# First MLP's low words partly by identity products, one spread for two, and new offsets in a fused attention and two-MLP kernel

## The chip, the cores and the metric

The kernel runs on one core of a Trainium2 chip. The metric is the device time of one execution in microseconds, as a median of several runs. The engines are PE (TensorE, matrix products; PEld is its loading of weights), DVE (VectorE), ACT (ScalarE), POOL (GpSimd) and SP (SyncE, which issues most DMAs).

## The reference

Three layers stand one behind another, for 4 batches of 768 tokens and 384 columns (8 heads of 48):

```python
# 1. delta-rule attention, token by token
k_n = k / (norm(k) + 1e-6)
for t in range(S):
    y[t] = q[t] @ state
    state += beta[t] * outer(k_n[t], v[t] - k_n[t] @ state)
# 2. first MLP: a low-rank mixing of the tokens, then 384 -> 1536 -> 384
u = x + (x.T @ U @ V).T
x = u + maximum(u @ w_ch1, 0) @ w_ch2
# 3. second MLP: real part of a 2-d Fourier transform, layer norm, the same MLP
u = x + real(fft(fft(x, axis=1), axis=2))
x = u + maximum(layernorm(u) @ w_ch1, 0) @ w_ch2
```

All is float32. The kernel keeps that accuracy with pairs of f16 words: a value is a high word and a low word, and a product is three products (high with high, high with low, low with high).

## The kernel before

The kernel has no schedule of its own in its source. Each part is a generator (a stream) that yields the cost and the engine of its next operation before it issues it, and a planner, `Weave`, picks at build time among all streams the one whose next operation can start first by its model, with an offset for each stream (`PR0`, `PR`, `P2`, `ME`, `MX`, `MB0`, `MB` and the like) and a price for each engine (`PRICE`, `PRICE2`). The order of issue on each engine is therefore fixed when the kernel is built, and each engine works through its own list in that order. The planner's clocks `free["v"]`, `free["a"]`, `free["p"]` say when DVE, ACT and PE would be done with what was issued so far. `SPW` is an addition to the time that a DMA issue waits for another engine's result.

There are two phases. In `attention` the sequence is cut into 24 chunks (4 batches of 6 chunks of 128 tokens). For a chunk, `s_front` and `row_scales` scale keys and queries (with `norm` for the reciprocal root), `s_turn` transposes them by DMA, `s_prep_a` makes the products of keys with keys and queries, `s_split` splits them into words, `s_prep_b` (two lanes) and `s_prep_c` invert a triangular matrix block by block, and `s_solve` carries the state from chunk to chunk. `s_solve` posts ("sol", u) when chunk u is done; its result, vt, is written at L1087.

Beside this the streams of the first MLP run whenever they fit: `s_mix` (the low-rank mixing and the split into words), `s_moe1` (the MLP) and `s_out1`. What is left of them goes on into the second phase, `second`, with the transform (`s_fft`), the second MLP's weights and the second MLP (`s_moe2`).

Both MLPs are `s_mlp` (`wi` is 0 for the first one and 1 for the second). A tile has 384 tokens; there are 8 tiles and 12 steps for each, so 96 steps in each MLP. In a step, nine products of 384 columns (L1135) fill a bank ps_h in PSUM; ACT writes the high word hh = Relu(ps_h) (L1141); DVE writes the low word hl = max(ps_h, 0) - hh (L1148); and nine products (L1165) take the words of the step before into three banks acc. In the first MLP ps_h has a single bank, so the next step's first product waits for hl.

`spread` (L827) multiplies a compact matrix, repeated along the columns, by a mask: the tiles t (T02 and T11, 512 columns each) in `s_prep_c`, bd and nf (1024 columns) elsewhere. In `s_prep_c` T02 is used in the products ps_l, and T11, after a block of it was replaced, in ps_x. `norm` has on DVE a line for s0 times a factor plus a summand (L657) between a product (L655) and the sum s1 (L660). `s_split` has, for the first 8 chunks, what the change brings to the MLP: the products with a negative identity, idm, onto the bank (L813) and a second ACT pass over it (L815), which leaves the low word.

Of the kernel before, what the change touches and what calls it, by code (L numbers as in the profile page):

```python
# [9 lines left out]
F32 = mybir.dt.float32  # L10
F32R = mybir.dt.float32r
F16 = mybir.dt.float16
BF16 = mybir.dt.bfloat16
U32 = mybir.dt.uint32
ALU = mybir.AluOpType
ACTF = mybir.ActivationFunctionType
# [3 lines left out]
B, H, S, D = 4, 8, 768, 48  # L20
DM = 384
DFF = 1536
NC = S // 128
# [17 lines left out]
NP = 27  # L41
UA = 8
SPARE = 150.0
SPW = 0.0
PR0 = (-272, -129.0, -103.0, 119.0, -13, -79, 889, 238.0)
PR = (-20.0, -145.0, -187.0, -178, 362, 14.0, 310, -190)
ME = -49
MX = -607
MB = -561
MB0 = -600.0  # L50
P2 = (-261, 79, -1288, -22, -199, -243, 152, -346)
MP = 29
WB1 = -697
WB = -409
PRICE0 = {'p': 1.0, 'v': 3.16, 'a': 0.82, 'g': 0.1}
PRICE = {'p': 1.0, 'v': 0.35, 'a': 0.57, 'g': 0.19}
PRICE2 = {'p': 1.0, 'v': 4.28, 'a': 0.53, 'g': 0.45}
SC = 16.0
CQ, CV, CW, CF = 6, 10, 9, 9
CU = 5  # L60
# [134 lines left out]
def _v(n, rate=1):  # L195
    return 67 + n / (0.96 * rate)


def _a(n, psum=False):
    return (51 if psum else 93) + n / 1.2  # L200
# [10 lines left out]
class Builder:  # L211
# [306 lines left out]
    def attn_pools(self, ctx):  # L518
        tc, nc = self.tc, self.nc
        self.psb = ctx.enter_context(tc.tile_pool(name="psb", bufs=1, space=PSUM))  # L520
        self.psr = ctx.enter_context(tc.tile_pool(name="psr", bufs=1, space=PSUM))
        self.pss = ctx.enter_context(tc.tile_pool(name="pss", bufs=1, space=PSUM))
        self.ap1 = ctx.enter_context(tc.tile_pool(name="ap1", bufs=1))
        self.ap2 = ctx.enter_context(tc.tile_pool(name="ap2", bufs=2))

        kq = self.kq0 = self.ap1.tile([128, 2, H, D], F32, tag="kq", name="kq", bufs=NQ)
        for i, src in enumerate((self.k, self.q)):
            nc.sync.dma_start(kq[:, i], src[0, :, 0:128, :].rearrange("h p d -> p h d"))
        self.mask2 = self.ap1.tile([128, 128], F32, name="mask2")
        nc.sync.dma_start(self.mask2, self.cmask)  # L530
        mm = self.ap1.tile([128, 640], F16, name="mmask")
        nc.gpsimd.dma_start(mm, self.cmerge)
        self.mpair, self.mcol, self.mdiag = mm[:, 0:32], mm[:, 32:64], mm[:, 64:96]
        self.mbd = mm[:, 96:224].rearrange("p (j c) -> p j c", j=4)
        self.mlev = [mm[:, x:x + 128].rearrange("p (j c) -> p j c", j=4) for x in (224, 352)]
        self.mt02, self.mt11 = (mm[:, x:x + 64].rearrange("p (j c) -> p j c", j=2) for x in (480, 544))
        self.betaT = self.ap1.tile([128, B * H * NC], F32, name="betaT")
        bv = self.beta.rearrange("b h (c p) -> (b h c) p", p=128)
        for i in range(2):
            bst = self.keep.tile([128, 128], F32, tag="xn", name="bst", bufs=TB // 128)  # L540
            nc.sync.dma_start(bst[0:96], bv[96 * i:96 * i + 96, :])
            pt = self.psm.tile([128, 512], F32, tag="psm", name="ps_b")
            nc.tensor.transpose(pt[:, 0:96], bst[0:96, :], self.id32[0:96, 0:96])
            nc.vector.tensor_copy(out=self.betaT[:, 96 * i:96 * i + 96], in_=pt[:, 0:96])

        def zeros(n, shape, nm):
            ts = [self.ap1.tile(shape, F16, name=f"{nm}{i}") for i in range(n)]
            for t in ts:
                (nc.vector if nm[0] == "k" else nc.gpsimd).memset(t, 0.0)
            return ts  # L550

        self.id16 = self.ap1.tile([128, 128], F16, name="id16")
        nc.vector.tensor_copy(out=self.id16, in_=self.id32)
        self.ids = self.ap1.tile([128, 128], F16, name="ids")
        nc.vector.tensor_scalar(out=self.ids, in0=self.id32, scalar1=SC, scalar2=None, op0=ALU.mult)
        self.idm = self.ap1.tile([128, 128], F16, name="idm")
        nc.vector.tensor_scalar(out=self.idm, in0=self.id32, scalar1=-1.0, scalar2=None, op0=ALU.mult)

        self.kq16 = zeros(NQ, [128, 2, H, 2, 64], "kq16")
        self.kb16r = zeros(NK, [128, H, 2, 64], "kb16")  # L560
        self.Nfr = [self.ap1.tile([128, H, 128], F16, name=f"nf{i}") for i in range(NR)]
        self.bd = [self.ap1.tile([128, H, 128], F16, name=f"bd{i}") for i in range(4)]
        self.T02, self.T11 = (self.ap1.tile([128, H, 64], F16, name=f"t1{i}") for i in range(2))
        self.lanes = self.psb.tile([128, 2, H, 32], F32, name="lanes")
        self.X128 = zeros(1, [128, H, 64], "t")[0]
        self.Xm = zeros(1, [128, H, 32], "xm")[0]
# [78 lines left out]
    def norm(self, pool, ss, n, eps, scale=1.0):  # L645

        nc = self.nc
        s0 = pool.tile([128, n], F32, tag="n_s0", name="n_s0", bufs=1)
        yield {"a": 190}
        nc.scalar.activation(out=s0, in_=ss, func=ACTF.Sqrt, bias=self.tiny)  # L650
        t = pool.tile([128, n], F32, tag="n_t", name="n_t", bufs=1)
        yield {"v": 76}
        nc.vector.reciprocal(out=t, in_=s0)
        yield {"v": 76}
        nc.vector.tensor_tensor(out=t, in0=ss, in1=t, op=ALU.mult)  # L655
        yield {"v": 76}
        nc.vector.tensor_scalar(out=s0, in0=s0, scalar1=0.5 / scale, scalar2=eps / scale, op0=ALU.mult, op1=ALU.add)  # L657
        s1 = pool.tile([128, n], F32, tag="n_s1", name="n_s1", bufs=NK + 2 if pool is self.ap2 else 2)
        yield {"v": 76}
        nc.vector.scalar_tensor_tensor(out=s1, in0=t, scalar=0.5 / scale, in1=s0, op0=ALU.mult, op1=ALU.add)  # L660
        r1 = pool.tile([128, n], F32, tag="n_r1", name="n_r1")
        yield {"v": 76}
        nc.vector.reciprocal(out=r1, in_=s1)
        return s1, r1
# [230 lines left out]

    def s_prep_c(self):
        nc = self.nc
        T02, T11, X128, Xm = self.T02, self.T11, self.X128, self.Xm
        Q = [slice(32 * i, 32 * i + 32) for i in range(4)]
        for u, _ in self.each():  # L900
            yield ("b", u)
# [2 lines left out]
            GPh = self.un[u]["GPh"]  # L904
            Tc, Nc = self.un[u].pop("TN")
            Nf = self.Nfr[u % NR]
            yield from self.spread(T02, Tc, self.mt02)
            t = yield from self.take()
            ps = self.psu.tile([128, H, 64], F32, tag="psu", name="ps_l")
            yield self.pe(H, 64)  # L910
# [7 lines left out]
            t = yield from self.take()  # L918
            pz = self.psu.tile([128, H, 32], F32, tag="psu", name="ps_z")
            yield self.pe(H, 32)  # L920
            for h in range(H):
                nc.tensor.matmul(pz[:, h, :], Nf[:, h, :], Xm[:, h, :], start=True, stop=True)
            yield from self.spread(T11, Tc, self.mt11)
            self.wv.post("ce", u)
            Zs = self.ap2.tile([128, H, 32], F16, tag="Zs", name="Zs", bufs=1)
            yield from self.cp(Zs, pz, 256, "chain", psum=True)
# [5 lines left out]
            t = yield from self.take()  # L932
            ps = self.psu.tile([128, H, 64], F32, tag="psu", name="ps_x")
# [177 lines left out]
    def s_mlp(self, wi, count, n_, np_, psm):  # L1111
# [5 lines left out]
        for s in range(count * steps + 1):  # L1117
            n, p = divmod(s, steps)
            if n < count:
                if p == 0:  # L1120
                    yield ("u", wi, n)
                    u = self.u[wi, n]
                pool, tag = psm[s % len(psm)]
                ps = pool.tile([128, np_, n_], F32, tag=tag, name="ps_h")
                for i in range(np_):
                    f = np_ * p + i
                    yield ("weights", wi, "w1", f // 3)
                    w1h, w1l = self.wt[wi, "w1h", f // 3], self.wt[wi, "w1l", f // 3]
                    fs = slice(128 * (f % 3), 128 * (f % 3) + 128)
                    m = 0  # L1130
                    for k in range(KD):
                        if k % MG == 0:
                            yield {"q": 3 * MG * (n_ / 2.4 + 2.5)}, "par"
                        for w, x in ((w1h, 0), (w1h, 1), (w1l, 0)):
                            nc.tensor.matmul(ps[:, i, :], w[:, k, fs], u[x][:, k, :], start=(m == 0), stop=(m == 3 * KD - 1))  # L1135
                            m += 1
                yield "join"
                hh = self.keep.tile([128, np_, n_], F16, tag="hh", name="hh", bufs=2)
                hl = self.keep.tile([128, np_, n_], F16, tag="hl", name="hl", bufs=2)
                yield {"a": _a(np_ * n_, True)}, "side"  # L1140
                nc.scalar.activation(out=hh, in_=ps, func=ACTF.Relu)  # L1141
            if pend and pend[0][1] == 0:
                ac = []
            for i in range(np_):
                for d in range(KD):
                    if n < count and i * KD + d == (np_ * KD // 3 if pend else 0):
                        yield {"v": _v(np_ * n_)}, "side"
                        nc.vector.scalar_tensor_tensor(out=hl, in0=ps, scalar=0.0, in1=hh, op0=ALU.max, op1=ALU.subtract)  # L1148
                    if not pend:
                        continue  # L1150
                    pn, f, xh, xl = pend[i]
# [526 lines left out]
```

## Time and profile before

| | us |
|---|---|
| median of 3 runs | 1105.74 (1100.96 to 1106.52) |
| profiled execution, its own time | 1102.48 |
| its span, first to last instruction | 1100.7 |
| PE busy | 945.0 (86%) |
| DVE busy | 747.5 (68%) |
| ACT busy | 555.1 (50%) |
| POOL busy | 330.0 (30%) |
| mean granted PE clock | 0.944 |

The shares are means over stages that differ, so they are read by stretch. Products on PE are pipelined: the duration of one in a table is longer than the distance to the next one. A granted clock of 1.00 is 2.4 GHz and one of 0.50 is 1.2 GHz; a mean between them is a share of time at either.

### The profile page before, as it was taken

Reading aid. Unit: us, or ns where it says so; the run is one execution under the profiler, and the core shown is the slowest. Engines: PE = TensorE matmul, PEld = TensorE weight load, DVE = VectorE, ACT = ScalarE, POOL = GpSimd, SP = SyncE. Lnnn points to the kernel's source line nnn. Section 1 sums busy time; section 2 is a strip of 40 time slices with the busy share of each in tenths; the row PEclk is TensorE's granted clock in tenths of the full one; section 3 lists DMA queues with packets and bytes.
Section 4 is the critical chain, followed back from the end, with each engine's and each line's share of the span. In section 5 each row is a group of like instructions: output and inputs, shape, how many; then the busy total and the mean of one; then the engine's idle time right before and its main releaser. Section 6 shows DMA issues by size and latency. Waiting matters only on the chain. (4 is left out here: it accounts for less than half of the span.)

```text
span 1100.7 us, 25252 instructions
## 1 busy us (share of the span) xinstructions
PE 945.0 (86%) x10127; PEld 633.1 (58%) x10127; DVE 747.5 (68%) x1735; ACT 555.1 (50%) x1372; POOL 330.0 (30%) x320
## 2 busy tenths in 40 slices
PE   0477776679999989998999889789999999999998
PEld 0255555446666656665666456455767575665665
DVE  7678689778989889897886377764425543544432
ACT  5589797766665655675553144356522221222221
POOL 4231323015343223543410450355353612102010
PEclk9998796579999999999999899899999999999999
DMA  9987976518555395476312455531102211212210
GB/s 229 221 172 151 203 159 139 122 41 150 115 102 110 86 181 118 86 147 121 71 38 66 131 154 142 150 94 29 56 11 67 78 29 37 65 29 58 58 37 22
DMA packets 226142, 112.18 MB, mean 102 GB/s; under 512 B 194396, under 2 KB 214184, under 8 KB 226024
## 3 DMA queue, kind: packets, MB, share of 16 engines
q1 hardware_dynamic: 223576, 103.32, 42.6%
q0 software_dynamic: 2448, 7.24, 2.2%
q8 instruction: 79, 1.29, 0.5%
q14 instruction: 39, 0.32, 0.1%
HBM read 55.63 MB, written 14.16 MB: 63 GB/s over the span
## 5 line engine op out<-in xcount | busy, mean ns | idle before, releaser
L1165 PE MATMUL acc<-w2s,hh 128*128 128x384 f16 x1152 | 288.2, 333 | 0.0
L1135 PEld LDWEIGHTS <-w1s 128*128 128x128 f16 x1728 | 164.5, 99 | 125.8 <-issue 24.7
L1148 DVE SCALAR_TENSOR_TENSOR hl<-ps_h,hh 128x384 f16<-128x384 f32 x192 | 106.1, 553 | 178.8 <-ACT hh L1141 176.7
L1141 ACT ACTIVATE hh<-ps_h 128x384 f16<-128x384 f32 x192 | 94.0, 489 | 241.7 <-PE ps_h L1135 238.7
L1165 PE MATMUL acc<-w2s,hl 128*128 128x384 f16 x576 | 190.9, 331 | 3.2 <-DVE hl L1148 3.2
L1135 PE MATMUL ps_h<-u,w1s 128*128 128x384 f16 x864 | 174.9, 336 | 21.3 <-DVE hl L1148 16.0
L1135 PE MATMUL ps_h<-uh,w1s 128*128 128x384 f16 x864 | 157.5, 326 | 0.0
L1165 PEld LDWEIGHTS <-hh 128*128 128x128 f16 x1152 | 108.7, 100 | 63.6 <-issue 4.6
L248 POOL TENSOR_TENSOR GPl<-g,GPh 128x512 f16<-128x512 f32 x63 | 79.6, 1264 | 172.2 <-ACT GPh L241 167.3
L847 PEld LDWEIGHTS <-bd 128*128 128x128 f16 x1728 | 71.9, 99 | 55.7 <-DVE bd L827 21.5
L1165 PEld LDWEIGHTS <-hl 128*128 128x128 f16 x576 | 57.2, 99 | 43.3 <-DVE hl L1148 4.0
L780 PE MATMUL ps_g<-K,BT 128*128 128x256 f16 x192 | 57.0, 316 | 17.1 <-DMA K<-KT 17.1
L779 PE MATMUL ps_g<-KT,BT 128*128 128x256 f16 x192 | 56.2, 309 | 14.0 <-ACT GPl L815 6.9
L248 POOL TENSOR_TENSOR pair<-x1f,pair 128x384 f16<-128x384 f32 x24 | 21.9, 915 | 132.1 <-ACT pair L1524 132.1
L786 DVE TENSOR_TENSOR g<-ps_g,mask 128x512 f32<-128x512 f32 x64 | 43.6, 682 | 11.1 <-PE ps_g L780 9.9
L248 POOL TENSOR_TENSOR pm<-xq 97x768 f32<-97x768 f32 (+1 forms) x16 | 28.8, 1816 | 65.2 <-DVE u L1296 45.9
L241 ACT ACTIVATE GPh<-g 128x512 f16<-128x512 f32 x61 | 38.0, 625 | 19.4 <-DVE g L786 19.1
L248 POOL TENSOR_TENSOR kb<-kq,rb 128x384 f32<-128x384 f32 x22 | 18.6, 846 | 91.6 <-ACT rh L1013 26.5
L780 PEld LDWEIGHTS <-BT 128*128 128x128 f16 x192 | 20.5, 107 | 36.8 <-DMA K<-KT 19.1
L827 DVE TENSOR_TENSOR bd<-Xc,mmask 128x1024 f16<-128x1024 f16 x48 | 36.8, 769 | 6.9 <-ACT Xc L881 6.5
L248 POOL TENSOR_TENSOR kq<-kq,kq 128x384 f16<-128x384 f32 x43 | 40.5, 962 | 3.3 <-ACT GPh L241 1.7
L847 PE MATMUL lanes<-R,bd 128*128 128x32 f16 x768 | 35.1, 180 | 5.5 <-ACT R L241 2.9
(261 smaller groups left out, 1927.1 us busy)
## 6 DMA issues: line engine op xcount, KB each, us to landing
wst<-in_moe_w_ch_dram SPq DMA_DIRECT2D x51, 384.0 KB
K<-KT SPq DMA_DIRECT2D x48, 256.0 KB
kq<-in_k_dram SPq DMA_DIRECT2D x24, 192.0 KB
kq<-in_q_dram SPq DMA_DIRECT2D x24, 192.0 KB
vt<-in_v_dram SPq DMA_DIRECT2D x24, 192.0 KB
xnd<-vt SPq DMA_DIRECT2D x24, 192.0 KB
xn<-xnd SPq DMA_DIRECT2D x24, 192.0 KB
x1d<-u SPq DMA_DIRECT2D x24, 192.0 KB
```

What stands on the lines that cost most here:

```text
L241: self.nc.scalar.activation(out=out, in_=in_, func=ACTF.Copy)
L248: (self.nc.vector if eng == "v" else self.nc.gpsimd).tensor_tensor(out=out, in0=in0, in1=in1, op=op)
L779: nc.tensor.matmul(o, BT[:, h, :], KT[:, :, h, :], start=i == 0, stop=False, skip_group_check=True)
L780: nc.tensor.matmul(o, BT[:, h, :], K2[:, :, h, :], start=False, stop=True, skip_group_check=True)
L786: nc.vector.tensor_tensor(out=g32.rearrange("p i (a t) -> p (i a) t", a=2), in0=ps.rearrange("p i (a t) -> p (i a) t", a=2), in1=self.mask ...
L827: self.nc.vector.tensor_tensor(out=dst.rearrange("p h (j c) -> p h j c", j=n), in0=x, in1=mask[:, None, :, :].to_broadcast(shape), op=ALU. ...
L847: nc.tensor.matmul(ps[:, h, :], lhs[:, h, :], rhs[:, h, :], start=plus is None, stop=plus is None or h == H - 1)
L1135: nc.tensor.matmul(ps[:, i, :], w[:, k, fs], u[x][:, k, :], start=(m == 0), stop=(m == 3 * KD - 1))
L1141: nc.scalar.activation(out=hh, in_=ps, func=ACTF.Relu)
L1148: nc.vector.scalar_tensor_tensor(out=hl, in0=ps, scalar=0.0, in1=hh, op0=ALU.max, op1=ALU.subtract)
L1165: nc.tensor.matmul(acc, h[:, ds_], w, start=(f == 0 and j == 0), stop=(f == KF - 1 and j == 2))
```

## The change

In the first MLP, as long as the last attention chunk but one is not solved, and where the planner's clock of DVE is later than that of ACT minus 469 ns (`HB`), the low word is made in another way: PE adds -hh to the bank with an identity product, and ACT writes Relu of what is left. So that the rest is not negative where ps_h is positive, hh is taken as Relu of ps_h times 1 - 2^-11 in the first MLP. Elsewhere the low word stays on DVE.

The two spreads for T02 and T11 become one of 1024 columns into one tile, T1, at the place of the first. In `norm` the factor and summand go from DVE to ACT, into a tile of their own, beside the DVE work. The offsets `SPW`, `MX`, `MB0`, three of `P2` and ACT's price in `PRICE2` have new values.

```diff
-SPW = 0.0
+SPW = -111
-MX = -607
+MX = -651
-MB0 = -600.0
-P2 = (-261, 79, -1288, -22, -199, -243, 152, -346)
+MB0 = -541
+P2 = (-261, 130, -1288, -22, -199, -233, 152, -320)
+HB = -469
-PRICE2 = {'p': 1.0, 'v': 4.28, 'a': 0.53, 'g': 0.45}
+PRICE2 = {'p': 1.0, 'v': 4.28, 'a': 0.64, 'g': 0.45}
...
-        yield {"v": 76}
-        nc.vector.tensor_scalar(out=s0, in0=s0, scalar1=0.5 / scale, scalar2=eps / scale, op0=ALU.mult, op1=ALU.add)
+        yield {"a": 190}, "par"
+        h = pool.tile([128, n], F32, tag="n_h", name="n_h", bufs=1)
+        nc.scalar.activation(out=h, in_=s0, func=ACTF.Copy, scale=0.5 / scale, bias=eps / scale)
+        yield "join"
...
-        nc.vector.scalar_tensor_tensor(out=s1, in0=t, scalar=0.5 / scale, in1=s0, op0=ALU.mult, op1=ALU.add)
+        nc.vector.scalar_tensor_tensor(out=s1, in0=t, scalar=0.5 / scale, in1=h, op0=ALU.mult, op1=ALU.add)
...
-            yield from self.spread(T02, Tc, self.mt02)
+            yield from self.spread(T1, Tc, self.mt)
...
-            yield from self.spread(T11, Tc, self.mt11)
...
-                nc.scalar.activation(out=hh, in_=ps, func=ACTF.Relu)
+                nc.scalar.activation(out=hh, in_=ps, func=ACTF.Relu, scale=1.0 if wi else 1.0 - 2.0 ** -11)
...
-                        yield {"v": _v(np_ * n_)}, "side"
-                        nc.vector.scalar_tensor_tensor(out=hl, in0=ps, scalar=0.0, in1=hh, op0=ALU.max, op1=ALU.subtract)
+                        if not wi and ("sol", B * NC - 2) not in self.wv.mark and self.wv.free["v"] > self.wv.free["a"] + HB:
+                            yield {"p": np_ * n_ / 2.4 + 2.5}, "side"
+                            nc.tensor.matmul(ps[:, 0, :], self.idm, hh[:, 0, :], start=False, stop=True, skip_group_check=True)
+                            yield {"a": _a(np_ * n_, True)}, "side"
+                            nc.scalar.activation(out=hl, in_=ps, func=ACTF.Relu)
+                        else:
+                            yield {"v": _v(np_ * n_)}, "side"
+                            nc.vector.scalar_tensor_tensor(out=hl, in0=ps, scalar=0.0, in1=hh, op0=ALU.max, op1=ALU.subtract)
```

## Rows read from the trace of the kernel before

**Rows 1.** Busy time by stretch: start:end, length, engines (x count), PE clock, DMA share, GB/s.

```profile
core 0: us, PE busy (x) PEld busy (x) DVE busy (x) ACT busy (x) POOL busy (x), PEclk, DMA share, GB/s
0.00:220.00 220.00, 133.39 (x2013) 95.83 (x2014) 173.53 (x412) 168.69 (x436) 61.44 (x72) 0.84 0.82 175
...
250.00:550.00 300.00, 271.98 (x4155) 194.94 (x4152) 264.49 (x590) 182.36 (x453) 114.34 (x104) 0.98 0.58 116
550.00:600.00 50.00, 47.53 (x786) 34.24 (x785) 39.80 (x96) 24.78 (x60) 3.48 (x3) 1.00 0.19 49
600.00:700.00 100.00, 84.09 (x555) 53.03 (x554) 62.88 (x122) 34.20 (x97) 26.52 (x22) 0.88 0.52 151
700.00:800.00 100.00, 94.12 (x586) 59.33 (x585) 54.98 (x140) 57.08 (x132) 50.24 (x49) 0.98 0.24 61
800.00:1101.00 301.00, 292.29 (x1833) 181.66 (x1830) 128.13 (x324) 69.06 (x153) 69.26 (x68) 1.00 0.17 45
...
250.00:590.00 340.00, 309.69 (x4798) 222.31 (x4795) 297.78 (x671) 204.50 (x506) 117.82 (x107) 0.98 0.53 107
```

**Rows 2.** One line's instructions, L1087: duration ns min/median/max, first and last start us.

```profile
L1087 ACT ACTIVATE vt<-ps_s,dn x24: 562/581/583, 82.2 to 606.4; 128x384 f32<-128x384 f32 x24
```

**Rows 3.** The chain that ended last, in order of time: start us, us, what.

```profile
934.67 1.46 PE ps_h L1135 x9
936.13 1.46 PE acc L1165 x9
```

**Rows 4.** One line's instructions, L1148, from 0 to 596 us.

```profile
L1148 DVE SCALAR_TENSOR_TENSOR hl<-ps_h,hh x53: 512/548/558, 223.6 to 594.1; 128x384 f16<-128x384 f32 x53
```

**Rows 5.** Groups by line and shape, 250:590 us: busy us, mean ns | idle before, releaser.

```profile
L1148 DVE SCALAR_TENSOR_TENSOR hl<-ps_h,hh 128x384 f16<-128x384 f32 x49 | 26.7, 545 | 1.8 <-ACT hh L1141 1.7
L1141 ACT ACTIVATE hh<-ps_h 128x384 f16<-128x384 f32 x49 | 24.0, 489 | 15.1 <-PE ps_h L1135 14.4
L827 DVE TENSOR_TENSOR t<-Tc,mmask 128x512 f16<-128x512 f16 x30 | 17.7, 590 | 0.1
L827 DVE TENSOR_TENSOR nf<-Nc,mmask 128x1024 f16<-128x1024 f16 x15 | 13.6, 906 | 0.0
...
L657 DVE TENSOR_SCALAR n_s<-n_s 128x9 f32<-128x9 f32 x11 | 3.0, 276 | 0.0
```

**Rows 6.** Lines L813 and L815, and what their engines sat idle for (us, times).

```profile
L813 PE MATMUL ps_g<-GPh,idm x32: 376/584/634, 36.3 to 174.6; 128*128 128x512 f16 x32
...
  ACT GPh L806: 2.0, 3
...
L815 ACT ACTIVATE GPl<-ps_g x32: 574/592/602, 37.1 to 175.3; 128x512 f16<-128x512 f32 x32
...
  PE ps_g L813: 2.9, 7
```

**Rows 7.** Lines L1183 and L650: duration ns min/median/max, first and last start us.

```profile
L1183 ACT ACTIVATE few<-few x8: 188/204/206, 204.0 to 712.9; 128x3 f32<-128x3 f32 x8
...
L650 ACT ACTIVATE n_s<-ssq,few x24: 289/303/307, 7.8 to 517.6; 128x9 f32<-128x9 f32 x24
```

**Rows 8.** Timeline of PE: start us, us, what [idle before, releaser].

```profile
634.61 2.36 PE L1135 MATMUL ps_h<-u,w1s 128*128 128x384 f16 x9 [3.95 <-DVE hl L1148]
...
692.76 3.06 PE L1135 MATMUL ps_h<-u,w1s 128*128 128x384 f16 x9 [5.13 <-DMA u<-xn]
```

**Rows 9.** Waits in 250:590 us: us in total, times, longest us.

```profile
ACT hh L1141 <- PE ps_h L1135: 14.4, 17, 3.0
```

More of the change, by code (lines that the diff above doesn't have):

```diff
@@ L535, in attn_pools @@
         self.mlev = [mm[:, x:x + 128].rearrange("p (j c) -> p j c", j=4) for x in (224, 352)]
-        self.mt02, self.mt11 = (mm[:, x:x + 64].rearrange("p (j c) -> p j c", j=2) for x in (480, 544))
+        self.mt = mm[:, 480:608].rearrange("p (j c) -> p j c", j=4)
         self.betaT = self.ap1.tile([128, B * H * NC], F32, name="betaT")
@@ L562, in attn_pools @@
         self.bd = [self.ap1.tile([128, H, 128], F16, name=f"bd{i}") for i in range(4)]
-        self.T02, self.T11 = (self.ap1.tile([128, H, 64], F16, name=f"t1{i}") for i in range(2))
+        self.T1 = self.ap1.tile([128, H, 128], F16, name="t1")
         self.lanes = self.psb.tile([128, 2, H, 32], F32, name="lanes")
@@ L897, in s_prep_c @@
         nc = self.nc
-        T02, T11, X128, Xm = self.T02, self.T11, self.X128, self.Xm
+        T1, X128, Xm = self.T1, self.X128, self.Xm
+        T02, T11 = T1[:, :, 0:64], T1[:, :, 64:128]
         Q = [slice(32 * i, 32 * i + 32) for i in range(4)]
```

## The prediction

> **What bounds the kernel now.** I read the busy time of each engine by stretch first [rows 1]. The reader is to see four stages. Up to about 220 us only the attention runs: PE is busy 133.4 of 220 us, at a granted clock of 0.84. From there to 606 us, where the last chunk's result is written [rows 2], attention and the first MLP share the engines. From 600 to 800 us the leftover of the first MLP, the transform and the second MLP's weights overlap: PE idles 15.9 and 5.9 us. After 800 us PE is busy 292.3 of 301 us. The chain that ended last says what that busy means [rows 3]: nine products into ps_h, nine into acc, 1.46 us each, back to back. One product of 384 columns so takes 1.46 / 9 = 0.162 us there, and an MLP step 2.93 us. Behind 800 us nothing but fewer products would shorten the span.
>
> The stage that the change works on is the second. There the two engines stand close together: in 250 to 550 us DVE is busy 264.5 of 300 us (88%), PE 272.0 (91%), ACT only 182.4 (61%). The last stretch of the same stage is a comparison that the trace gives for free: in 550 to 600 us, where less vector work is left, DVE is at 39.8 of 50 (80%) and PE at 47.5 (95%) [rows 1]. So PE fills up when DVE gets lighter, by about four points for nine. That DVE is the late engine for the low words shows in the waits too: DVE idled 1.7 us in all for the 49 high words hh (its row in rows 5), so hh had nearly always long been there when DVE came to hl. The first MLP there moves at one step in (594.1 - 223.6) / 52 = 7.1 us [rows 4], far from the 2.93 us of its products, so its own chain of ps_h, hh, hl has room.
>
> **Low words by an identity product.** Up to the solve of the last chunk but one (its result is written at about 595 us) 53 low words are made [rows 4]. Each one that takes the new way loses a DVE operation of 0.545 us [rows 5] and gains a product of 384 columns, 0.162 us by rows 3, and a Relu on ACT, which by the hh of the same shape and source costs 0.489 us [rows 5]. The nearest thing in the kernel is the attention's own identity product with its second ACT pass, 32 times before 175 us: the ACT pass takes 0.592 us for 512 columns, ACT waited 2.9 us in all for the products, and PE 2.0 us in all for the first copies [rows 6]. How many low words go the new way isn't in the trace: the rule compares the planner's own clocks of DVE and ACT. DVE is the fuller engine, and the rule allows it to be 0.469 us early still, so I take three quarters, 40, with 20 and 53 as ends.
> - DVE: -40 x 0.545 = -21.8 us (-10.9 to -28.9).
> - ACT: +40 x 0.489 = +19.6 us.
> - PE: +40 x 0.162 = +6.5 us (3.2 to 8.6). This part is not hidden: PE is at 91%.
>
> What waits behind: the product stands in PE's order behind the first third of the pending acc products; it waits for hh, and all later products wait behind it. Behind the second Relu on ACT stand the chain's copies. By rows 6, per use, that is 2.0 / 32 = 0.06 us of PE and 2.9 / 32 = 0.09 us of ACT, so 2.5 us of PE for 40: an upper end, as that stretch had a fuller ACT (168.7 of 220 us); I take it into the range, not the sum. The factor on hh's Relu costs nothing: same operation.
>
> ScalarE: Activation LUTs of the Trainium skill says, in its Rules for kernel authors, that a Relu belongs on VectorE, which can be about three times as fast per element. This trace doesn't agree for operands in PSUM: 0.489 us on ACT against 0.545 on DVE [rows 5]. By the rule the Relus would cost 40 x 3 x 0.545 = 65 us of ACT and bring it to 270 of 340 us, as full as DVE becomes; I give that no chance, as the row is of the same shape, source and function.
>
> **One spread in place of two.** Two operations of 512 columns (0.590 us each) become one of 1024, for which the nearest row, also from a repeated source, says 0.906: 2 x 0.590 - 0.906 = 0.274 us less per chunk [rows 5]. For 15 chunks in 250 to 590 us that is -4.1 us of DVE. The first product waits 0.3 us longer for its operand; the second spread's place behind it falls away, so the chain is even.
>
> **One step of the norm on ACT.** In the stretch it is an operation of 0.276 us, 11 times: -3.0 us of DVE [rows 5]. On ACT the nearest rows are a 3-column operation with a plain factor (0.204 us) and the Sqrt of the same 9 columns (0.303 us) [rows 7]: +2.2 to +3.3 us. It runs beside two DVE operations; if ACT is busy just then, DVE's queue stands behind the join for at most one ACT operation, say 0.6 us x 11 = 6.6 us. I take nothing, and keep it for the range.
>
> **The sum for 250 to 590 us.** DVE falls from 297.8 [rows 1] by 21.8 + 4.1 + 3.0 = 28.9 us to 268.9, which is 79% of 340 us: the share of 550 to 600 us. ACT rises to some 227 us (67%). PE's work becomes 309.7 + 6.5 = 316.2 us. With PE as full as it was at that DVE share, 95.1%, the stretch takes 316.2 / 0.951 = 332.5 us: -7.5 us. At PE's old 91.1% it takes 347.1: +7.1. I take the former, by the row whose DVE share matches.
>
> **Before 220 us** the spread and the norm save DVE some 9 x 0.274 + 13 x 0.276 = 6 us of 173.5; it isn't the bound alone there, with ACT at 168.7 of 220. The chunk's chain gets a little of it: -1 (0 to -6). The new offsets shift when the mixing starts; no row prices an order that isn't there.
>
> **Between 600 and 800 us** there are holes, among them 5.13 us until a transposed u lands, at half clock behind it, and 3.95 us for one hl [rows 8]. A shared stage shorter by 7.5 us leaves one step more (one per 7.1 us) for them, 2.93 us of products, so some -2 (0 to -3). The new offsets redraw this order as well: between -16 (the holes of 600 to 700 us closed) and as much the other way.
>
> Sum: -7.5 - 1 - 2 = -10.5 us. The profiled execution lasted 1102.5 us (span 1100.7); it goes to 1092.0. The median of the three runs, 1105.7, lies 3.2 above it, so the median goes to 1095.2; I say 1095.
>
> **Rivals.**
> - Little changes. Few words take the new way (20), and what is freed on DVE sits where the solve's own chain is the limit: PE gains one point instead of four: (309.7 + 3.2) / 0.92 = 340.1, so 0, with the -2 from elsewhere 1104. For it: ACT's waits for PE, 14.4 us for hh alone [rows 9], tell that latency counts too. Against it: DVE's 88%.
> - PE doesn't fill up at all: its 95% at the end came from the work that was left there, not from the lighter DVE. Then the products are a pure load: +7.1, 1112.8. It decides at PE's share: below 316.2 / 340 = 93.0% the change costs time in this stretch.
> - PE stands behind the identity product. If each of the 40 waits out a whole hh (0.489 us), because ACT, now 6 points fuller, comes later to it, PE loses 19.6 us and -10.5 turns into +9: 1115. It decides at 10.5 / 40 = 0.26 us of wait each. Against it: 0.06 us each [rows 6]. PSUM — Partial Sum Buffer of the Trainium skill (Engine vs sequencer instructions) says that ACT's queue is strictly first in, first out and that products start in program order, so such a wait could not be passed. The 3.95 us by which PE stood idle for one hl [rows 8] agree.
> - The holes of 600 to 700 us close with the new offsets: up to -14 more than in the sum, 1081.
>
> **How the numbers follow.** Forecast (gain of 4 to 18 us) 0.49; holes closed as well 0.09; little changes 0.24; PE doesn't fill 0.12; PE behind the product 0.06. 0.5%, about what a measurement of this kernel can tell from no change, is 5.5 us. The weak end of the forecast lies within it, and the two bad cases reach above it in most of their span: faster 0.56, same 0.27, slower 0.17. The range is 1078 to 1113: below, the closed holes with most of their gain; above, PE not filling; the 1115 case is left out.
>
> **What would show it.** Low words on ACT: 40 of 53 (20 and 53 are the ends), with 0.49 us each. DVE near 80% and PE near 95% between 250 and 550 us. The last chunk's result before 606.4 us [rows 2] by some 8 us. The spread at 0.9 us, 24 times. PE's waits for hh at the identity products under 3 us. Wrong it would be if PE stays at 91% with a lighter DVE, or if PE shows idle time before the identity products of 10 us and more; if the time moved while the shared stage did not, the offsets did it.

## The result, and the profile after

The changed kernel takes 1077.13 us (median of 4 runs, 1074.86 to 1081.55) against 1106.13 us beside it: a ratio of 0.9746, 95% interval 0.9694 to 0.9798. By the ratio that is 28 us, 2.5% faster, nearly three times the forecast of 10.5 us, and 0.9 us below the low end of the range. The profiled execution was the slowest of the four, 1081.55 us with a span of 1079.8; against the profiled execution of before it gained 20.9 us, and the ledger below is of that.

Busy time by stretch of the changed kernel, columns as in [rows 1]:

```profile
core 0: us, PE busy (x) PEld busy (x) DVE busy (x) ACT busy (x) POOL busy (x), PEclk, DMA share, GB/s
0.00:220.00 220.00, 135.76 (x2112) 97.29 (x2113) 176.75 (x406) 174.07 (x455) 61.68 (x72) 0.88 0.81 175
...
250.00:550.00 300.00, 274.74 (x4324) 199.01 (x4321) 256.77 (x575) 193.21 (x483) 113.92 (x101) 0.99 0.58 113
...
600.00:700.00 100.00, 88.30 (x536) 54.50 (x535) 66.84 (x143) 41.55 (x119) 21.71 (x17) 0.97 0.52 145
700.00:800.00 100.00, 95.48 (x594) 59.94 (x593) 50.20 (x114) 51.10 (x113) 56.85 (x56) 0.98 0.22 54
...
250.00:590.00 340.00, 313.97 (x4898) 226.19 (x4896) 282.03 (x635) 210.44 (x524) 113.92 (x101) 0.99 0.53 104
```

The stretch that the forecast rested on, 250 to 590 us, hardly changed: PE from 309.7 to 314.0 us, of which the identity products alone are 36 x 0.162 = 5.8. DVE fell by 15.8 us, not by 28.9 (the section on the prediction shows why). Where the time went is told by when chunks and steps were done. First the line that writes a chunk's result, for the sixth and seventh chunk, of before (L1087) and after (L1090); the columns are those of [rows 2]:

```profile
L1087 ACT ACTIVATE vt<-ps_s,dn x2: 563/572/581, 189.8 to 240.1; 128x384 f32<-128x384 f32 x2
```

```profile
L1090 ACT ACTIVATE vt<-ps_s,dn x2: 564/570/577, 182.1 to 222.4; 128x384 f32<-128x384 f32 x2
```

The seventh chunk came 17.7 us earlier, and 7.7 us of that stood already at the sixth, before the first identity product of the changed kernel at 212.5 us. The last one came at 589.1 instead of 606.4 [rows 2], 17.3 earlier, and the first MLP stood at the same step then, as hh of before (L1141) and after (L1144) up to the last chunk's result say:

```profile
L1141 ACT ACTIVATE hh<-ps_h x55: 470/491/498, 219.6 to 602.9; 128x384 f16<-128x384 f32 x55
```

```profile
L1144 ACT ACTIVATE hh<-ps_h x55: 469/491/492, 212.0 to 587.0; 128x384 f16<-128x384 f32 x55
```

So the whole gain of the attention phase, 17 us, was made before 222 us, and from there to the last chunk both kernels need some 366.5 us and do the same steps. The place is the attention alone and the start of the first MLP. These are the instructions on ps_h until 250 us, of before from 212 us and of after from 205 us:

```profile
L1135 PE MATMUL ps_h<-u,w1s x30: 326/524/528, 216.9 to 249.7; 128*128 128x384 f16 x30
L1141 ACT ACTIVATE hh<-ps_h x3: 473/491/491, 219.6 to 242.0; 128x384 f16<-128x384 f32 x3
L1148 DVE SCALAR_TENSOR_TENSOR hl<-ps_h,hh x3: 548/551/558, 223.6 to 245.9; 128x384 f16<-128x384 f32 x3
```

```profile
L1138 PE MATMUL ps_h<-u,w1s x63: 322/326/524, 208.6 to 247.9; 128*128 128x384 f16 x63
...
L1152 PE MATMUL ps_h<-hh,idm x6: 322/324/336, 212.5 to 248.9; 128*128 128x384 f16 x6
L1154 ACT ACTIVATE hl<-ps_h x6: 471/477/491, 213.9 to 249.3; 128x384 f16<-128x384 f32 x6
L1157 DVE SCALAR_TENSOR_TENSOR hl<-ps_h,hh x1: 548/548/548, 242.3 to 242.3; 128x384 f16<-128x384 f32 x1
```

In before the first hh begins at 219.6 us and takes 0.49, and the first hl begins at 223.6: DVE came 3.5 us late to it. By 250 us PE has done 63 products into ps_h instead of 30, most of them at the fast clock (median 326 ns against 524). In the second phase the changed kernel reaches the second MLP 29.9 us earlier, and needs 8.9 us more from there (328.4 against 319.5); PE is busy 5.8 us longer in that part (316.9 against 311.1). The last hh of the first MLP and the first of the second, of before and after, on the timeline of ACT:

```profile
773.30 0.49 ACT L1141 ACTIVATE hh<-ps_h 128x384 f16<-128x384 f32 x1 [1.10 <-PE ps_h L1135]
...
781.20 0.48 ACT L1141 ACTIVATE hh<-ps_h 128x384 f16<-128x384 f32 x1
```

```profile
745.88 0.49 ACT L1144 ACTIVATE hh<-ps_h 128x384 f16<-128x384 f32 x1 [0.28 <-PE ps_h L1138]
...
751.35 0.48 ACT L1144 ACTIVATE hh<-ps_h 128x384 f16<-128x384 f32 x1
```

The ledger of the profiled executions: up to the last chunk -17.3, from there to the second MLP -12.6 (162.2 instead of 174.8), behind that +8.9; sum -20.9.

### The profile page after: what moved, and what is told of

Same layout as the page of the kernel before. It is cut to its first block, busy times and chain, and to the rows that moved or that the text cites. A ratio compares the mean times of both kernels' runs of the same rounds, so it can differ in the third digit from the quotient of the medians.

```text
span 1079.8 us, 25291 instructions
## 1 busy us (share of the span) xinstructions
PE 936.7 (87%) x10169; PEld 627.0 (58%) x10169; DVE 728.3 (67%) x1663; ACT 567.1 (53%) x1422; POOL 331.1 (31%) x318
## 5 line engine op out<-in xcount | busy, mean ns | idle before, releaser
L1174 PE MATMUL acc<-w2s,hh 128*128 128x384 f16 x1152 | 283.7, 328 | 3.5 <-DVE u L1305 3.5
L1144 ACT ACTIVATE hh<-ps_h 128x384 f16<-128x384 f32 x192 | 93.8, 488 | 224.5 <-PE ps_h L1138 220.9
L1157 DVE SCALAR_TENSOR_TENSOR hl<-ps_h,hh 128x384 f16<-128x384 f32 x150 | 83.3, 555 | 170.1 <-ACT hh L1144 169.4
L1174 PE MATMUL acc<-w2s,hl 128*128 128x384 f16 x576 | 188.6, 327 | 4.2 <-DVE hl L1157 2.8
L1138 PE MATMUL ps_h<-u,w1s 128*128 128x384 f16 x864 | 172.1, 333 | 9.3 <-DVE hl L1157 7.4
L783 PE MATMUL ps_g<-K,BT 128*128 128x256 f16 x192 | 53.5, 300 | 14.4 <-DMA K<-KT 14.3
L782 PE MATMUL ps_g<-KT,BT 128*128 128x256 f16 x192 | 53.2, 296 | 8.4 <-DMA KT<-kq 3.4
L249 POOL TENSOR_TENSOR pair<-x1f,pair 128x384 f16<-128x384 f32 x24 | 22.3, 930 | 113.6 <-ACT pair L1533 113.6
L249 POOL TENSOR_TENSOR kb<-kb,kb 128x384 f16<-128x384 f32 x22 | 21.9, 995 | 57.8 <-ACT kb L242 48.8
L1003 PEld LDWEIGHTS <-GPh 128*128 128x128 f16 x768 | 31.0, 98 | 13.5 <-issue 9.2
L783 PEld LDWEIGHTS <-BT 128*128 128x128 f16 x192 | 19.9, 103 | 29.6 <-DMA K<-KT 17.3
L242 ACT ACTIVATE GPh<-g 128x512 f16<-128x512 f32 x52 | 32.4, 622 | 8.3 <-DVE g L789 8.3
```

Source lines behind the costliest of these rows:

```text
L242: self.nc.scalar.activation(out=out, in_=in_, func=ACTF.Copy)
L249: (self.nc.vector if eng == "v" else self.nc.gpsimd).tensor_tensor(out=out, in0=in0, in1=in1, op=op)
L782: nc.tensor.matmul(o, BT[:, h, :], KT[:, :, h, :], start=i == 0, stop=False, skip_group_check=True)
L783: nc.tensor.matmul(o, BT[:, h, :], K2[:, :, h, :], start=False, stop=True, skip_group_check=True)
L1003: nc.tensor.matmul(ps[0:m, h, :], lf(h), x[:, h, :], start=start and i == 0 and h == 0, stop=stop and not whole and i == len(terms) - 1 an ...
L1144: nc.scalar.activation(out=hh, in_=ps, func=ACTF.Relu, scale=1.0 if wi else 1.0 - 2.0 ** -11)
```

## The experiments

Two rival theories stood at the start: the lighter DVE (code), or the order that the new offsets draw. A third, that the offsets were fitted to one order, came with them.

**Offsets alone.** The kernel before with the new values:

```diff
-SPW = 0.0
+SPW = -111
...
-PRICE2 = {'p': 1.0, 'v': 4.28, 'a': 0.53, 'g': 0.45}
+PRICE2 = {'p': 1.0, 'v': 4.28, 'a': 0.64, 'g': 0.45}
```

> The kernel before with the seven new offset values alone (SPW, MX, MB0, three of P2, ACT's price of the second phase); no identity product, two spreads, norm on DVE. The changed kernel stood at 1077 us against 1106, and its sixth to seventh chunk came 17.7 us earlier. Theory A (the offsets redraw the start of the first MLP and the transition, and that is most of the gain): 1080 to 1092, with the seventh chunk's result (L1087) near 225 us instead of 240. Theory B (the lighter DVE is the cause, by identity products, spread and norm): 1100 to 1110, seventh chunk near 240 us.

1118.26 us, ratio 1.016 (1.012 to 1.020): slower. Both theories missed: the offsets alone lose. The seventh chunk stood at 240.2 us, as before.

**Code alone.** The changed kernel with the old offsets (the diff above turned around).

> All three edits of the code (identity products, one spread, norm's step on ACT) with the old offset values. Theory B (lighter DVE): 1080 to 1092, and the seventh chunk's result near 222 us. Theory A (offsets): 1095 to 1106, and the seventh chunk near 240 us. Theory C (each alone does little, as the order is redrawn with every edit and the offsets fit the code): both this one and the one with the offsets alone lie within 8 us of 1106.

1082.89 us, ratio 0.9834 (0.9794 to 0.9875), in the range of the theory of the lighter DVE. But the seventh chunk came at 236.5 us, not at 222. By then five steps of the first MLP had begun (counted as hh written by ACT), where it is two at the seventh chunk of the kernel before and of the changed one. At 2.93 us of products a step [rows 3], 236.5 us with five steps are about as far as 227.7 with two: 12 us ahead of the kernel before, 5 behind the changed one. With the code, the new early offsets put the chunk first and the old ones the steps.

**Identity products alone**, on the kernel before:

```diff
-                nc.scalar.activation(out=hh, in_=ps, func=ACTF.Relu)
+                nc.scalar.activation(out=hh, in_=ps, func=ACTF.Relu, scale=1.0 if wi else 1.0 - 2.0 ** -11)
...
+                        if not wi and ("sol", B * NC - 2) not in self.wv.mark and self.wv.free["v"] > self.wv.free["a"] + HB:
```

> The kernel before with the identity products and second Relu alone (and the factor on hh), old offsets, two spreads, norm on DVE. The prediction's step gave -7.5 us from 250 to 590 us for about 40 products: 1098. If PE doesn't fill up with a lighter DVE: +7, 1113. Until the first MLP starts at about 217 us it must run as the kernel before, seventh chunk near 240 us.

1099.56 us, ratio 1.0001 (0.9977 to 1.0025): nothing. The trace says where it went. The last chunk came at 591.4 us with 55 steps done, 15.0 us earlier than in the kernel before at the same step; 3.6 us of that stood already at the sixth chunk, before any identity product, so 11 to 15 us are theirs. But the way from there to the second MLP took 186.6 us instead of 174.8. That is one hole on PE, in the first MLP, until a transposed u landed; in the kernel before PE waits 5.13 us there [rows 8]:

```profile
687.65 3.04 PE L1136 MATMUL ps_h<-u,w1s 128*128 128x384 f16 x9 [16.80 <-DMA u<-xn]
```

**No identity products**, all else as in the changed kernel:

```diff
-                        if not wi and ("sol", B * NC - 2) not in self.wv.mark and self.wv.free["v"] > self.wv.free["a"] + HB:
+                        if False:
```

> The changed kernel with every low word on DVE (the condition never holds; the factor on hh stays); one spread, norm's step on ACT and the new offsets stay. Theory B with identity products as the main part: 1084 to 1092 or more (the prediction's -7.5 us lost). Theory A or spread and norm as the main part: 1075 to 1084. DVE between 250 and 590 us should rise from 282 of 340 us towards 300.

1092.68 us, ratio 0.9942 (0.9919 to 0.9965), some 2% behind the changed kernel: by the time, as the first theory has it. DVE stood at 297.0 us in 250 to 590, as expected. But the seventh chunk came at 223.1 us without any identity product, and the last one at 604.1 with 60 steps done. So spread, norm and early offsets alone bring the seventh chunk forward, and five steps more, of 2.93 us each [rows 3], make up for the later last chunk. What the identity products add to these edits came behind the last chunk, at this one order of the second phase: between 600 and 700 us PE is busy for 81.3 us at a clock of 0.91, in the changed kernel for 88.3 at 0.97.

**Identity products in the first tile alone, and in all others alone:**

```diff
-                        if not wi and ("sol", B * NC - 2) not in self.wv.mark
+                        if not wi and n == 0 and ("sol", B * NC - 2) not in self.wv.mark
```

```diff
-                        if not wi and ("sol", B * NC - 2) not in self.wv.mark
+                        if not wi and n > 0 and ("sol", B * NC - 2) not in self.wv.mark
```

> The changed kernel with identity products in the first tile's 12 steps alone (from some 210 to 290 us); all later low words on DVE. Theory D (the identity products earn their gain where the first MLP starts, 200 to 250 us, as DVE comes 3 to 7 us late to the first low words there, PE idles and its clock is granted at half; later they are about even): 1075 to 1083, within 6 us of the changed kernel, and PE at 26 of 30 us in 220 to 250. Theory B' (the relief of DVE counts all along the shared stage): 1084 to 1092, near the kernel without any identity product.

> The complement: the first tile's low words on DVE, identity products from the second tile on (some 30). Theory D: the start is lost, 1084 to 1092, PE near 22 of 30 us in 220 to 250. Theory B': 1077 to 1084.

1093.32 us (0.9944, 0.9923 to 0.9966) and 1098.53 us (0.9987, 0.9964 to 1.0011). By the time, theory D missed: the first kernel is about as slow as the one without identity products, as theory B' has it, and the second is slower than either theory allowed. But the start went as theory D says. Stretch 220 to 250 us of the kernel with the first tile alone, of the one with all others alone, and of the next experiment:

```profile
220.00:250.00 30.00, 26.07 (x318) 17.48 (x319) 24.18 (x54) 23.15 (x60) 9.30 (x9) 1.00 0.55 110
```

```profile
220.00:250.00 30.00, 23.23 (x225) 14.96 (x224) 23.02 (x52) 19.99 (x49) 7.75 (x8) 0.79 0.30 70
```

```profile
220.00:250.00 30.00, 22.27 (x248) 14.30 (x245) 23.85 (x53) 21.57 (x53) 8.83 (x8) 0.83 0.40 80
```

With the low words of the start on ACT, PE has the clock of 1.00 all through and is busy for 26 us; with them on DVE 0.79 and 23 us. At the last chunk the first kernel stood at 600.3 us with 60 steps done, the second at 585.3 with 54: at 2.93 us a step that is 585.7 and 588.2 at 55 steps, so neither is behind the changed kernel (589.1), and up to there these runs can't tell the two theories apart. What both lost, they lost behind 735 us, in a hole that the kernel with one offset moved by one has too (below).

**The product, with the Relu on DVE:**

```diff
-                            yield {"a": _a(np_ * n_, True)}, "side"
-                            nc.scalar.activation(out=hl, in_=ps, func=ACTF.Relu)
+                            yield {"v": _v(np_ * n_)}, "side"
+                            nc.vector.tensor_scalar(out=hl, in0=ps, scalar1=0.0, scalar2=None, op0=ALU.max)
```

> The changed kernel with the identity products kept, but the Relu behind them on DVE (0.5 us each) instead of ACT: PE does the added work, DVE isn't lightened, one more handover in each step. If DVE's lightening is what the identity way gives: worse than the kernel without identity products, 1092 to 1102. If the added products help by keeping PE active at the start (higher granted clock in 200 to 250 us): 1078 to 1086.

1105.73 us, ratio 1.007 (1.0049 to 1.0091): worse than with no identity product at all, and than the first theory allowed. In the third row above PE has 22.3 us and a clock of 0.83, though the products are there. At the last chunk it stood at 578.0 us with only 48 steps: brought to 55 steps that is 598.5, 9 us behind the kernel with no identity product, and as much behind the changed one. So in this kernel the product and its handover cost some 9 us, and the Relu's step from DVE to ACT earns them back. That is one order, and one execution differs from another by up to 5 us at this place (below), so the direction is shown and the size is rough. More products for PE didn't help by themselves.

**One offset moved by one:**

```diff
-ME = -49
+ME = -48
```

> The changed kernel with one offset that the change doesn't touch moved by 1 (ME, from -49 to -48): the order is drawn anew and no work is added or taken. It measures what a redrawn order alone is worth. Theory C (the offsets are fitted to this very order): 1080 to 1095, later by up to 1.5%. Otherwise 1074 to 1080.

1101.57 us, ratio 1.0022 (1.0002 to 1.0042): the whole gain is gone, later than even theory C said. The work is not quite the same, against what was expected: 46 low words went the new way, instead of 42. Yet this kernel was not behind at the last chunk (583.0 us, 54 steps) and ahead between 600 and 700 us (PE busy 93.1 us against 88.3). It lost all in one hole. The waits above 1 us of PE between 735 and 770 us on its timeline, and the stretch itself:

```profile
740.50 0.38 PE L1326 MATMUL ps_f<-few,ones 128*128 128x1 f32 x2 [2.09 <-DVE few L1322]
763.74 5.81 PE L1138 MATMUL ps_h<-uh,w1s 128*128 128x384 f16 x18 [22.85 <-DMA uh<-pair]
...
735.00:770.00 35.00, 10.05 (x45) 5.27 (x44) 17.53 (x39) 12.06 (x29) 25.78 (x24) 0.61 0.29 78
```

The last low word of the first MLP was written at 736 us, and the first transposed input of the second landed at 764: from 708 to 727 us the last products of the first batch's transform had stood one by one between those of the first MLP in PE's order. DVE came to the last of them at 727.9 us, in the changed kernel at 702.2:

```profile
727.90 0.36 DVE L1465 TENSOR_TENSOR dm<-ps_q,dp 128x193 f32<-128x193 f32 x1 [0.17 <-ACT dp L1463]
```

```profile
702.23 0.36 DVE L1465 TENSOR_TENSOR dm<-ps_q,dp 128x193 f32<-128x193 f32 x1 [0.81 <-ACT dp L1463]
```

The two kernels with a part of the identity products have a hole at the same place: from the first MLP's last hh to the second's first it is 16.3 us with the first tile alone and 31.3 with all others, against 5.5 in the changed kernel.

**The same, with the transform put ahead:**

```diff
-ME = -49
+ME = -48
...
-P2 = (-261, 130, -1288, -22, -199, -233, 152, -320)
+P2 = (-261, 130, -1288, -94, -199, -145, 152, -320)
```

> The kernel with ME at -48 had PE further at 725 us than the changed kernel, and lost it in one hole of 22.9 us (741 to 764) where PE waited for the second MLP's first transposed input. Here ME stays at -48, and two offsets of the second phase put the transform ahead and the first MLP back (P2's fourth value from -22 to -94, its sixth from -233 to -145); nothing changes before 580 us. Theory E (the time is set by which comes last, the first MLP's end or the second MLP's first input, and the code's gain is real behind it): no hole over 8 us, 1070 to 1082. Theory C (the gain was a lucky order): 1090 to 1102.

1070.41 us, ratio 0.9732 (0.9698 to 0.9765): as theory E said. The hole is gone:

```profile
735.00:770.00 35.00, 31.54 (x203) 21.64 (x201) 18.51 (x50) 21.77 (x50) 18.00 (x19) 0.95 0.13 35
```

**One offset of the second phase, on the kernel before and on the changed one:**

```diff
-P2 = (-261, 79, -1288, -22, -199, -243, 152, -346)
+P2 = (-40, 79, -1288, -22, -199, -243, 152, -346)
```

```diff
-P2 = (-261, 130, -1288, -22, -199, -233, 152, -320)
+P2 = (-170, 130, -1288, -22, -199, -233, 152, -320)
```

> The kernel before with one offset of the second phase, the one of the second MLP's input (P2's first value, -261 to -40), and no edit of the code. It asks what offsets picked anew alone can give, without the code. Theory C: 1075 to 1090. Theory E: nothing is won, since the kernel before has its first MLP's end last and not the input: 1092 to 1104.

> The changed kernel with the same offset moved (P2's first value, -261 to -170): the first MLP comes a little before the input of the second. Theory E: 1068 to 1080, about the changed kernel. Theory C: 1085 to 1100.

1090.97 us (0.9930, 0.9892 to 0.9967) and 1075.14 us (0.9783, 0.9753 to 0.9813). The kernel before gains 0.7% by an offset alone, a little more than theory E allowed; the changed one came out as theory E said. With one such offset moved in each, the changed code stays 16 us ahead, and the table below shows where: 14.9 us at the last chunk, while the second phases are alike (484.2 and 484.6).

**The old values for the second phase in the changed kernel** (three of P2 and ACT's price; the early offsets stay new):

> The changed kernel with the old values for the second phase (three of P2, ACT's price there); the same order as the changed kernel until some 580 us. It asks what these four values are worth on top of the code and the three early offsets: theory E 1078 to 1086, theory C 1090 to 1102.

1068.90 us, ratio 0.9717 (0.9683 to 0.9751): none of the theories had it faster. The new values of the second phase bring nothing; with the old ones the kernel is at least as fast, though the intervals overlap. Against the code alone (1082.89), which has the same second-phase values, the three early offsets are worth 14 us by the time. At the last chunk it is only some 2.5 us (590.0 against 592.5 at 55 steps); the rest is the order of the second phase.

Steps and chunks put the runs side by side (times of the profiled executions, in us; the second phase begins at the last chunk; one execution of one order differs from another by up to 5 us: the sixth chunk, until which the identity products alone change nothing, came at 186.2 us with them and at 189.8 without, and the last chunk of the two kernels with ME by one, which have one order until some 600 us, at 583.0 and 588.3):

| kernel | 7th chunk | last chunk | steps by then | second phase |
|---|---|---|---|---|
| before | 240.1 | 606.4 | 55 | 494.3 |
| before, input's offset moved | 239.2 | 605.0 | 55 | 484.2 |
| offsets alone | 240.2 | 626.0 | 59 | 493.4 |
| identity products alone | 237.2 | 591.4 | 55 | 503.2 |
| code alone | 236.5 | 589.6 | 54 | 493.6 |
| no identity products | 223.1 | 604.1 | 60 | 486.7 |
| changed | 222.4 | 589.1 | 55 | 490.7 |
| changed, input's offset moved | 221.2 | 590.1 | 55 | 484.6 |
| changed, second phase's offsets old | 221.5 | 590.0 | 55 | 480.0 |
| ME by one | 221.0 | 583.0 | 54 | 515.3 |
| ME by one, transform ahead | 224.3 | 588.3 | 54 | 484.3 |

A step is 2.93 us of products [rows 3], so 60 steps at 604.1 us are about as far as 55 at 589.4. Up to the last chunk, then, the identity products alone give 11 to 15 us, spread and norm with the new early offsets some 17, and all of them together 17: they buy the same slack and don't add. The new offsets on the old code lose there (626.0 with 59 steps, about 614 with 55). The second phase is a matter of order: among the kernels with 54 or 55 steps by then, which have nearly the same work left, it varies from 480.0 to 515.3 us, and the kernel before, too, gains 10 us of it by one offset.

## Why the prediction was right or wrong

- **The direction was right, the size too small by a factor of 2.7, and the place wrong.** 42 low words went the new way, where 40 were taken; that DVE was the engine to relieve agrees with the kernel with the Relu left on DVE, which gains nothing.
- **The prices were right.** The changed kernel's groups in 250 to 590 us:

```profile
L1144 ACT ACTIVATE hh<-ps_h 128x384 f16<-128x384 f32 x48 | 23.5, 490 | 21.8 <-PE ps_h L1138 21.0
L1154 ACT ACTIVATE hl<-ps_h 128x384 f16<-128x384 f32 x36 | 17.6, 489 | 12.8 <-PE ps_h L1152 12.6
L830 DVE TENSOR_TENSOR t<-Tc,mmask 128x1024 f16<-128x1024 f16 x15 | 12.6, 838 | 0.1
L659 ACT ACTIVATE n_h<-n_s 128x9 f32<-128x9 f32 x11 | 2.3, 207 | 0.0
```

  0.489 us for the second Relu (0.489 taken), 0.84 for the wide spread (0.906), 0.207 for the norm's step (0.204 to 0.303). The same Relu left on DVE took 0.551 us (median), so ACT was the cheaper engine for it, as the prediction read from a neighbouring operation. The factor of three that the prediction cites from ScalarE: Activation LUTs of the Trainium skill (Rules for kernel authors) is stated there for bf16 and single-source operations; the rows here are of f32 operands in PSUM, so they don't contradict it. PE waited 1.0 us in all for hh before the 42 identity products, so the rival of the blocked queue falls; ACT waited 12.6 us for the products, 0.30 each instead of 0.09, without harm.
- **The step that failed first is "PE as full as at that DVE share"** for 250 to 590 us, a term of -7.5. PE went from 91.1% to 92.3%, not to 95.1%, below the 93.0% at which the rival "PE doesn't fill up" put the point of decision, and from the seventh chunk to the last the kernel kept its 366 us. DVE fell by 15.8 us and not by 28.9, so it didn't reach the share of 550 to 600 us; and that row differs in more than DVE's share. The edits saved on DVE what the sum said: hl 20.1 us, the spread 5.1, the norm's line 3.0. What the sum had at nothing is the rest of DVE's and ACT's work: copies of the attention may go to either engine, the planner picks the engine when it builds the order, and in the changed kernel it gave DVE 46 instead of 22 of those into GPh, rh, Zs, U and d, 11.6 us more (32 of them in the kernel without identity products). ACT rose by 5.9 us only, not by some 22. One of these groups on DVE in 250 to 590 us, of before and after:

```profile
L243 DVE CAST GPh<-g 128x512 f16<-128x512 f32 x2 | 0.8, 418 | 0.0
```

```profile
L244 DVE CAST GPh<-g 128x512 f16<-128x512 f32 x12 | 5.0, 416 | 0.1
```

  On top of spread and norm the identity products gave nothing up to the last chunk; alone they gave 11 to 15 us there.
- **The term "before 220 us", -1, was the main one**: -17.7 by the seventh chunk. Part of it is the relief of DVE before the first MLP: all ten kernels with spread and norm have the sixth chunk at 181.5 to 184.1 us, the four without at 186.2 to 189.8, so these two edits give some 6 us there, all that they save on DVE by the prediction's own count and the far end of its range. The other 10 us came with the start of the first MLP, between the sixth and the seventh chunk, which the prediction had no term for. The kernel without identity products (223.1 us) shows that spread, norm and the new early offsets are enough for them, and the offsets alone (240.2) that these are not. I had put the offsets aside, as no row prices an order that isn't there. With the old ones the code came to the last chunk nearly as early (592.5 against 589.1 at 55 steps).
- **The second phase**, -2, came out at -3.6 (490.7 against 494.3), by luck: not for the reason given (one step more for the holes; the steps were 55 and 55, and the prediction's sum for the shared stage kept all of its steps, so none was left over). The rival of closed holes, -14, has its mechanism in part: PE was busy 88.3 instead of 84.1 us between 600 and 700 us, and orders without a hole behind 735 us reach 480.0 and 484.3. That the new offsets of the second phase did it is refuted: the old ones do at least as well there.
- **"Little changes"** gave 1104, about no change, and that is what the identity products alone came to (1099.56, ratio 1.0001), but not by its mechanism: they won 11 to 15 us and lost them in a hole. The sign "if the time moved while the shared stage did not, the offsets did it" misled: the offsets alone lost, and the code alone won 1.7%. That the offsets alone could lose 18 us, and one unit of one offset 24, stood in none of the rivals; an order redrawn was priced in one stretch only, at 16 us either way.

What stays open: which of the three early offsets brings the seventh chunk forward, and what spread and norm give one by one, or, behind the sixth chunk, with the old offsets and no identity products (neither was tried). The kernel without identity products stands level with the changed one at the last chunk, and its second phase is some 11 us longer when both are brought to the same step (490.7 against 1090.8 - 589.4 = 501.4). It was run at one order of the second phase only. An order at which the two chains meet better is likely to be the reason, but not shown for this pair, so whether the identity products are worth anything on top of spread, norm and offsets is open too.

## What to carry to other kernels

Two edits that relieve the same engine buy the same slack: here each gave 11 to 17 us up to the last chunk, and both together 17. Where a planner may give work to either of two engines, work taken off one can come back in another form: count the copies before and after, and not only the operations that were moved. In a kernel whose order is worked out in advance, compare two versions at several orders each: one unit of an untouched offset cost the whole 2.5%, and both could be told apart only by landmarks (a chunk's result, the steps by then, the second part's start). Read a chunk's time and the steps together, as an order can trade one for the other. Where two chains meet, ask which comes last; as soon as the first MLP was faster, the second one's input was what had to be brought forward.

## What the runs showed of the hardware

Between 220 and 250 us PE was granted a clock of 0.72 in the kernel before, 0.79, 0.83 and 0.89 in the three kernels with spread, norm and new offsets where the low words of the start were still written by DVE, and 1.00 (0.99 in one) where ACT wrote them. So a start with late low words went with a lower clock: in the kernel before most products into ps_h ran at half of it (median 524 against 326 ns in the changed kernel). PE's own waits for hl were small there, 0.8 us until 260 us; it waited longer for other results, among them 3.15 us for Zs on ACT and 1.79 us for a t on DVE. In the hole of 22.9 us the clock of 735 to 770 us fell to 0.61, and the next 18 products took 5.81 us, where two times nine at the full clock take 2.92.
